# An attention and MLP kernel whose MLP weight splits are kept in DRAM: made in the first token block, loaded in the other three

## The chip, the core and the metric

The kernel runs on one core of one Trainium2 chip. The metric is the device time of one execution in microseconds (us). One core has TensorE (PE: matmuls, with the weight load PEld beside it), VectorE (DVE), ScalarE (ACT), GpSimd (POOL) and SyncE (SP), which here only issues DMAs. Each engine takes its instructions in the order of the program; an instruction that waits for another engine holds up all that stand behind it on its own.

## What is computed

Two branches over the same 2,048 tokens of width 576, mixed by a gate per token:

```python
q, k, v = split(x @ wqkv)              # 32 heads of 18
a = softmax(q @ k.T * 18**-0.5) @ v @ wo
b = gelu(layernorm(x) @ w1 + b1) @ w2 + b2   # 576 -> 4608 -> 576
g = sigmoid((x * gate_w).sum(-1))
out = g * a + (1 - g) * b
```

All is float32. The kernel multiplies with float32r operands and keeps the accuracy by writing an operand as two parts: `hi`, the value rounded to float32r, and `lo`, what is left. A product of two such operands takes three matmuls (hi·hi, hi·lo, lo·hi).

## The kernel before, in words

**Stages.** A first stage (up to about 200 us) makes q, k, v and the layer-normed x (`y_scr`) and stores them in DRAM. Then attention and MLP run interleaved. A last stage multiplies by `wo` and mixes.

**Attention** goes through 32 units (a pair of heads, half of the queries), each in 16 steps: 512 steps. In a step PE makes two rounds of scores for the row maximum (`ps`, L176; DVE reduces them, L178), two pairs of score matmuls (`pss`, L213; four matmuls per step) that ACT turns into exponentials (`p`, L215), and one product with v (L228). `pss` has one buffer, so the next pair waits for the exponential before. At the end of a unit the sums are loaded into a tile `dn` by DMA (L242), and four slots later DVE takes their reciprocal (L251); the negated maxima of the next unit go by DMA from `mr` into two rows of `qa`.

**MLP.** Tokens come in 4 blocks of 512; d_ff = 4608 in 36 chunks of 128, 4 chunks to a group, so 9 groups per block and 18 pairs of chunks. `h_pair(q)` (L339) is 54 matmuls (L350) for a pair of chunks; its result goes through a GELU of five steps shared by ACT (L363, L383, L385) and POOL (`plus`, `parts`: `zz`, `hh`, `hl`, all at line L136), which ends in the two parts `hh` and `hl` of the hidden values. `outs(i)` (L424) is eight `out_unit`s of 24 matmuls (L403) for a group. `outs` waits, by yielding, until the parts of its group stand in `HT` (L429).

**Weights.** A raw pair of w1 is loaded into `r1` (L288), a raw pair of w2 into `r2` (L293), one buffer each. `split` (L301) makes two background jobs of each tile: `first` writes hi on POOL (or ACT for the first ones), `second` subtracts on POOL. The tiles `w` hold both parts: three buffers for w1 (`wp1`), four for w2 (`wp2`). This is done for each of the 72 pairs, that is, for the same 18 pairs four times over.

**What sets the order.** Every step makes four calls of `run_due` (L122); each call is a slot. A slot runs what `defer` put there, and pops one background job from `bg` when the estimated POOL load is under `SLOT`. `fill` (L867) puts MLP pieces into a step until the MLP is as far as its share of the steps, and stops at the end of a unit (`cut` 2) or where the MLP waits (`cut` 3). If a weight tile isn't made when a matmul needs it, `ready` (L313) pops jobs at once; this is called a forced split below. The order of each engine is fixed by this when the program is built. SP issues all loads and stores but those of the output, in this order too.

Of the kernel before, what the change touches and what calls it, by code (L numbers as in the profile page):

```python
# [8 lines left out]
F32 = mybir.dt.float32  # L9
F32R = mybir.dt.float32r  # L10
# [6 lines left out]
P = 128  # L17
S = 2048
D = 576
# [4 lines left out]
NB = 4  # L24
# [4 lines left out]
NFC = F // P  # L29
# [10 lines left out]
WAIT = 0.25  # L40
NSL = 1
SLOT = 950.0
R2 = 1
AHEAD = 1
TOTAL = NB * NG * (G // 2 * 27 * 231 + 8 * 3 * G * 131)
PRO = 36e3
# [11 lines left out]
def gated_mix_kernel(ctx: ExitStack, tc: tile.TileContext, x, wqkv, wo, w1, b1, w2, b2, gate_w, out):  # L58
    nc = tc.nc
# [4 lines left out]
    dram = ctx.enter_context(tc.tile_pool(name="dram", bufs=1, space=DRAM))  # L64
# [3 lines left out]

    qk_scr = dram.tile([2, 2 * D, S], F32, name="qk_scr")
    v_scr = dram.tile([NT, P, NPAIR, VW], F32, name="v_scr")  # L70
    y_scr = dram.tile([NB, 2, 9, 64, TB], F32, name="y_scr")
    ot_scr = dram.tile([2, D, S], F32, name="ot_scr")
    dn_scr = dram.tile([2 * NPAIR, 2, HALF], F32, name="dn_scr")
# [28 lines left out]
    def x_tile():  # L102
        return xp.tile([P, 4 * 640], F32, name="x")
# [4 lines left out]
    def dma_r(queue, dst, src):  # L108

        queue.dma_start(dst.bitcast(F32), src)  # L110


    slot = [0]
    later = []

    def defer(n, fn):
        later.append((slot[0] + n, fn))

    bg = []
    load = [0.0]  # L120

    def run_due():  # L122

        slot[0] += 1
        load[0] = max(load[0] - SLOT, 0.0)
        due = [f for s, f in later if s <= slot[0]]
        later[:] = [(s, f) for s, f in later if s > slot[0]]
        for f in due:
            f()
        if bg and load[0] < SLOT:  # L130
            bg.pop(0)()

    def pool_op(n, fn, *args, **kw):

        load[0] += n * (1.25 if fn == nc.gpsimd.tensor_scalar else 2.55)
        fn(*args, **kw)  # L136
# [132 lines left out]
    def mlp():  # L269
        W1, W2, HT = {}, {}, {}  # L270
        RAW = {}
        seq = [(tb, g) for tb in range(NB) for g in range(NG)]
        n = len(seq)
        npair = n * (G // 2)
        Y, ACC = {}, {}

        def chunk(q):

            i, m = divmod(q, G // 2)
            return i, m, seq[i][1] * G + 2 * m  # L280

        def load_w1(q, view=None):

            r1 = RAW[1, q] = rp.tile([P, 9, P], F32, name="r1") if view is None else view
            fc = chunk(q)[2]
            for h in range(2):
                src = w1[:, (fc + h) * P:(fc + h + 1) * P]
                nc.sync.dma_start(r1[64 * h:64 * h + 64], src.rearrange("(c p) n -> p c n", p=64))  # L288

        def load_w2(q):  # L290
            i, m, fc = chunk(q)
            r2 = RAW[2, q] = rp.tile([P, 2, D], F32, name="r2", bufs=R2)
            nc.sync.dma_start(r2, w2[fc * P:(fc + 2) * P, :].rearrange("(j p) d -> p j d", p=P))  # L293

        def rounded(dst, src, act=False):
# [2 lines left out]
                return  # L298
            pool_op(src.free_size(), nc.gpsimd.tensor_scalar, dst, src, 1.0, 1.0, op0=ALU.mult, op1=ALU.mult)

        def split(table, key, pool, shape, src, act):  # L301

            def first():
                t = table[key, "hi"] = pool.tile(shape, F32R, name=f"w{len(shape)}")
                rounded(t[:, 0], src(), act)

            def second():
                t = table.pop((key, "hi"))
                pool_op(src().free_size(), nc.gpsimd.tensor_tensor, t[:, 1], src(), t[:, 0].bitcast(F32), op=ALU.subtract)
                table[key] = (t[:, 0], t[:, 1])  # L310
            bg.extend([first, second])

        def ready(table, key):  # L313
            while key not in table:
                bg.pop(0)()
            return table[key]

        asked = [1]

        def prep(upto):  # L320

            while asked[0] <= min(upto, npair - 1):
                q = asked[0]
                asked[0] += 1
                split(W1, q, wp1, [P, 2, 9, P], lambda q=q: RAW[1, q], q == 1)
                if q + 1 < npair:
                    bg.append(lambda q=q: load_w1(q + 1))

        def prep_w2(i):
            for m in range(G // 2):  # L330
                q = i * (G // 2) + m
                for j in range(2):
                    split(W2, (q, j), wp2, [P, 2, D], lambda q=q, j=j: RAW[2, q][:, j, :], i == 0)
                if q + R2 < npair:
                    bg.append(lambda q=q: load_w2(q + R2))

        open_pairs = [0]

        def h_pair(q):  # L339

            i, m, fc = chunk(q)
            tb = seq[i][0]
            wt = ready(W1, q)
            del W1[q]
            ps = ps_w.tile([P, 2, TB], F32, name="psw")
            slots = [(w_, 0, c) for c in range(9) for w_ in (0, 1)] + [(0, 1, c) for c in range(9)]
            for k, (w_, s_, c) in enumerate(slots):
                for h in range(2):
                    r = slice(64 * h, 64 * h + 64)
                    nc.tensor.matmul(ps[:, h, :], wt[w_][r, c, :], Y[tb, s_][r, c, :], start=(k == 0), stop=(k == 26))  # L350
                if k == 26:
                    break
                if k % 3 == 2:
                    cut[0] = 1
                yield 231
                while k == 25 and open_pairs[0]:
                    cut[0] = 3
                    yield 0
            open_pairs[0] = 1
            zs = [zp.tile([P, TB], F32, name="z") for _ in range(2)]  # L360
            b = [b1t[:, fc + h:fc + h + 1] for h in range(2)]
            nc.vector.tensor_scalar(zs[1], ps[:, 1, :], b[1], None, op0=ALU.add)
            defer(2, lambda: nc.scalar.activation(zs[0], ps[:, 0, :], AF.Identity, bias=b[0]))  # L363
            for h in (1, 0):
                z = zs[h]
                w = zp.tile([P, TB], F32, name="zz", bufs=2)
                hh = hp.tile([P, TB], F32R, name="hh")
                hl = hp.tile([P, TB], F32R, name="hl")


                def plus(c, w, z):

                    pool_op(TB, nc.gpsimd.tensor_scalar, w, w, c, 1.0, op0=ALU.add, op1=ALU.mult)
                    pool_op(TB, nc.gpsimd.tensor_tensor, w, w, z, op=ALU.mult)

                def parts(w=w, z=z, hh=hh, hl=hl, h=h, j=2 * m + h):
                    plus(1.0, w, z)
                    rounded(hh, w)
                    pool_op(TB, nc.gpsimd.tensor_tensor, hl, w, hh.bitcast(F32), op=ALU.subtract)
                    HT[i, j] = (hh, hl)  # L380
                    if h == 0:
                        open_pairs[0] = 0
                defer(4, lambda w=w, z=z: nc.scalar.activation(w, z, AF.Square))  # L383
                defer(6 - h, lambda w=w, z=z: plus(GC0, w, z))
                defer(10 - 2 * h, lambda w=w: nc.scalar.activation(w, w, AF.Tanh, scale=GC1))  # L385
                defer(11 - 2 * h, parts)
            cut[0] = 2
            yield 231
# [53 lines left out]
        t = [pp.tile([P, 4 * TB], F32R, name="p")[:, :9 * P].rearrange("p (c n) -> p c n", c=9) for _ in range(2)]  # L442
        rounded(t[0], RAW[1, 0])
        nc.gpsimd.tensor_tensor(t[1], RAW[1, 0], t[0].bitcast(F32), op=ALU.subtract)
        W1[0] = t
        yield 1
        load_y(0, 1)
        load_w1(1)
        for q in range(R2):
            load_w2(q)  # L450
        q = 0
        for i in range(n + 1):
            for part in range(2):
# [21 lines left out]
    cut = [0]  # L475
# [15 lines left out]
    def filler(upto):  # L491

        while stream and spent[0] < upto:
            try:
                spent[0] += next(stream[0])
            except StopIteration:
                stream.pop(0)
        run_due()


# [212 lines left out]
    mstack = ExitStack()  # L713
    wp1 = mstack.enter_context(tc.tile_pool(name="m_w1", bufs=3))
    wp2 = mstack.enter_context(tc.tile_pool(name="m_w2", bufs=4))
    rp = mstack.enter_context(tc.tile_pool(name="m_raw", bufs=1))
    zp = mstack.enter_context(tc.tile_pool(name="m_z", bufs=3))

    hooks = []

# [1 line left out]
    def out_proj():  # L722
# [3 lines left out]
        raw = x_tile().rearrange("p (c n) -> p c n", n=640)[:, :, :D]  # L726

        def w_part(hl, c):
            return wbig[:, 5 * hl + c, :] if 5 * hl + c < 8 else wlast[:, c - 3, :]

        def split(c):
            src = raw[:, c % 4, :]
            nc.gpsimd.tensor_scalar(w_part(0, c), src, 1.0, 1.0, op0=ALU.mult, op1=ALU.mult)
            nc.gpsimd.tensor_tensor(w_part(1, c), src, w_part(0, c).bitcast(F32), op=ALU.subtract)
# [3 lines left out]
                nc.sync.dma_start(raw[64 * h:64 * h + 64, 0, :], wo[512:576, :])  # L738

        nc.sync.dma_start(raw, wo[0:512, :].rearrange("(c p) n -> p c n", p=P))  # L740
        bg.append(lambda: split(0))
        bg.append(load_last)
        for c in range(1, 5):
            bg.append(lambda c=c: split(c))
        OT, BT, done = {}, {}, {}

        def load_o(b):
# [73 lines left out]
        for b in range(NB):  # L821
# [7 lines left out]
            for t in range(4):  # L829
# [3 lines left out]
                for n in range(2):  # L833
                    cs = slice(n * ND, (n + 1) * ND)
                    ps = psum(ps_s1)
                    k = 0
# [99 lines left out]
```

## Time and profile before

| what | value |
|---|---|
| median of 3 runs | 2707.01 us (2706.32 to 2707.05) |
| the profiled execution's own time | 2706.99 us |
| its span | 2705.2 us, so 1.8 us lie around it |
| busy: PE, PEld, DVE | 2470.5, 1624.9, 1776.0 us |
| busy: ACT, POOL | 1331.7, 1435.3 us |
| mean granted TensorE clock | 0.955 |
| moved by DMA | 224.21 MB, 83 GB/s over the span |

The page shows the busy time of each engine and its share in 40 equal slices of the span. The group rows give, for a line and an operation, the names (out<-in), the shapes, the count, busy us and mean ns of one, and behind the bar the idle time of the engine just before them with what ended it. The view of waits gives engine, line, what was waited for, us in total, times, and the longest. The view of windows gives, for stretches of the span, the busy us of each engine with its count of instructions (x), the granted clock of TensorE, the share of the DMA engines and GB/s. Rows of the timeline begin with the start in us and the time that they took. Shares of PE are shares of modelled matmul ends; waits are inferred from semaphores.

### The profile page before, as it was taken

The numbers are of one execution on the slowest core, as the hardware profiler recorded it, in microseconds if no ns is written. First come the engines' busy times: TensorE is split into PE (matmuls) and PEld (weight loads), VectorE is DVE, ScalarE is ACT, GpSimd is POOL, SyncE is SP. The second block draws the span as 40 slices with busy tenths as digits, with TensorE's granted clock in tenths as the row PEclk, the third lists the DMA queues.
The fourth block names the chain that finished last, engine by engine and source line by source line (L and its number), as shares of the span: only waits on it lengthen the run. The fifth ranks groups of instructions, "written<-read, shape, count | busy, mean of one in ns | idle before, by whom it ended". The sixth has DMA issues, their size and how long they took to land. (4 is left out here: it accounts for less than half of the span.)

```text
span 2705.2 us, 50403 instructions
## 1 busy us (share of the span) xinstructions
PE 2470.5 (91%) x20585; PEld 1624.9 (60%) x20585; DVE 1776.0 (66%) x3178; ACT 1331.7 (49%) x1555; POOL 1435.3 (53%) x1337
## 2 busy tenths in 40 slices
PE   8996699999978799999978899999889898999868
PEld 7885556666645466666645566656555565666538
DVE  4544567787755577777756677777756676777514
ACT  3221155555545465555535555556545454665541
POOL 3003566675636467556446656566644656666410
PEclk9997799999989899999989999999999999999989
DMA  7676131212261313122251313131442221131145
GB/s 242 210 213 156 44 71 48 67 52 66 53 145 39 75 48 76 47 68 62 53 132 30 76 47 76 48 84 39 97 105 49 64 56 49 50 80 42 34 139 184
DMA packets 210935, 224.21 MB, mean 83 GB/s; under 512 B 55980, under 2 KB 144848, under 8 KB 208976
## 3 DMA queue, kind: packets, MB, share of 16 engines
q1 hardware_dynamic: 208400, 216.27, 30.9%
q10 hardware_dynamic: 2304, 4.72, 0.5%
q8 instruction: 162, 2.65, 0.4%
q14 instruction: 69, 0.57, 0.1%
HBM read 170.61 MB, written 54.26 MB: 83 GB/s over the span
## 5 line engine op out<-in xcount | busy, mean ns | idle before, releaser
L178 DVE TENSOR_REDUCE m<-ps 128x1 f32<-128x512 f32 x2048 | 1290.2, 682 | 393.4 <-PE ps L176 350.1
L215 ACT ACTIVATE p<-pss 128x1024 f32<-128x1024 f32 x1024 | 1049.7, 1025 | 980.8 <-PE pss L213 977.2
L213 PE MATMUL pss<-qa,ka 56*128 56x512 f32 x2048 | 560.0, 411 | 87.2 <-ACT p L215 82.5
L176 PE MATMUL ps<-ka,qa 54*128 54x512 f32 x2048 | 619.8, 454 | 21.7 <-DVE m L178 14.0
L403 PE MATMUL psw<-w,hh 64*128 64x288 f32 x4608 | 542.7, 300 | 52.3 <-POOL hh L136 21.4
L176 PEld LDWEIGHTS ps<-ka,qa 54*128 54x128 f32 x2048 | 311.7, 188 | 460.1 <-DVE x L411 209.6
L228 PE MATMUL ps<-p,vt 128*32 128x512 f32 x4096 | 554.3, 613 | 0.0
L350 PE MATMUL psw<-big,w 64*128 64x512 f32 x3834 | 516.7, 405 | 39.0 <-POOL w L136 27.5
L403 PEld LDWEIGHTS psw<-w,hh 64*128 64x128 f32 x4608 | 492.7, 190 | 81.5 <-POOL hh L136 23.3
L136 POOL TENSOR_SCALAR w<-r 128x576 fp32r<-128x576 f32 (+1 forms) x210 | 175.8, 837 | 604.5 <-DMA r<-in_B_w_dram 373.2
L403 PE MATMUL psw<-w,hl 64*128 64x288 f32 x2304 | 474.9, 299 | 10.6 <-POOL hl L136 10.5
L350 PEld LDWEIGHTS psw<-big,w 64*128 64x128 f32 x3834 | 391.3, 192 | 121.1 <-POOL w L136 32.4
L136 POOL TENSOR_TENSOR w<-r,w 128x576 fp32r<-128x576 f32 (+1 forms) x215 | 393.7, 1832 | 72.5 <-ACT w L297 56.1
L411 DVE SCALAR_TENSOR_TENSOR x<-psw,x 128x288 f32<-128x288 f32 x544 | 248.8, 457 | 248.2 <-PE psw L403 152.4
L403 PEld LDWEIGHTS psw<-w,hl 64*128 64x128 f32 x2304 | 380.4, 190 | 15.1 <-POOL hl L136 14.8
L136 POOL TENSOR_TENSOR zz<-zz,z 128x512 f32<-128x512 f32 x288 | 369.6, 1283 | 24.0
L213 PEld LDWEIGHTS pss<-qa,ka 56*128 56x128 f32 x2048 | 280.5, 189 | 133.8 <-ACT p L215 124.1
L136 POOL TENSOR_SCALAR zz<-zz 128x512 f32<-128x512 f32 x288 | 178.8, 621 | 164.1 <-ACT zz L383 118.9
L136 POOL TENSOR_TENSOR hl<-zz,hh 128x512 fp32r<-128x512 f32 x144 | 187.0, 1298 | 12.0
L228 PEld LDWEIGHTS ps<-p,vt 128*32 128x32 f32 x4096 | 81.3, 108 | 184.1 <-issue 183.9
L385 ACT ACTIVATE zz<-zz 128x512 f32<-128x512 f32 x144 | 89.8, 624 | 92.0 <-POOL zz L136 92.0
L136 POOL TENSOR_SCALAR hh<-zz 128x512 fp32r<-128x512 f32 x144 | 89.4, 621 | 12.6
(97 smaller groups left out, 1279.0 us busy)
## 6 DMA issues: line engine op xcount, KB each, us to landing
r<-in_B_w_dram SPq DMA_DIRECT2D x72, 576.0 KB
r<-in_B_w_dram SPq DMA_DIRECT2D x142, 288.0 KB
big<-y_scr SPq DMA_DIRECT2D x16, 1152.0 KB
qa<-qk_scr SPq DMA_DIRECT2D x192, 72.0 KB
ka<-qk_scr SPq DMA_DIRECT2D x96, 144.0 KB
qk_scr<-hh SPq DMA_DIRECT2D x36, 256.0 KB
qk_scr<-hl SPq DMA_DIRECT2D x36, 256.0 KB
v_scr<-vt SPq DMA_DIRECT2D x16, 416.0 KB
```

Of the source, the lines that this page charges most:

```text
L136: fn(*args, **kw)
L176: nc.tensor.matmul(ps, qa[r0:r0 + 54, t * P:(t + 1) * P], ka[r0:r0 + 54, kb * TB:(kb + 1) * TB], start=True, stop=True)
L178: nc.vector.tensor_reduce(M4[u][:, h, t, kb:kb + 1], ps, axis=AX.X, op=ALU.max)
L213: nc.tensor.matmul(ps[:, h, :], ka[r0:r0 + 56, kc * P:(kc + 1) * P], qa[r0:r0 + 56, qb * TB:(qb + 1) * TB], start=True, stop=True)
L215: nc.scalar.activation(PT[u, kc][:, qb], ps, AF.Exp, scale=SCALE)
L228: nc.tensor.matmul(OB[u][c:c + 32, :], v[:, kc, 19 * h:19 * h + 32], p[:, qb, h, :], start=(kc == 0), stop=(kc == NT - 1))
L350: nc.tensor.matmul(ps[:, h, :], wt[w_][r, c, :], Y[tb, s_][r, c, :], start=(k == 0), stop=(k == 26))
L385: defer(10 - 2 * h, lambda w=w: nc.scalar.activation(w, w, AF.Tanh, scale=GC1))
L403: nc.tensor.matmul(ps[:, h, :ND], h_[r, tok], w_[p_][r, cs], start=(k == 0), stop=(k == 3 * G - 1))
L411: nc.vector.scalar_tensor_tensor(dst, ps[:, h, :ND], 0.5, b2b[:, cs] if g == h == 0 else dst, op0=ALU.mult, op1=ALU.add)
```

## The change

The two parts of each weight pair are made in the first token block only (q below `NQ0` = 18). `second` stores the finished tile in DRAM (`w1_scr`, `w2_scr`); in blocks 2 to 4 `reload` loads a tile, both parts at once, straight into a `w` buffer, with no raw load and no POOL work. A job on a raw tile is popped only `LAND` = 8 slots after its load was issued, and holds up the jobs behind it until then; `ready` doesn't ask for that. The parts of the hidden values are entered in `HT` four slots after their last POOL instruction was issued. `filler` (used before the 512 steps and behind the MLP) stops when the MLP waits. There are four `z` buffers for three.

```diff
-R2 = 1
+LAND = 8
...
+    w1_scr = dram.tile([NFC // 2, P, 2, 9, P], F32, name="w1_scr")
+    w2_scr = dram.tile([NFC, P, 2, D], F32, name="w2_scr")
...
-        if bg and load[0] < SLOT:
-            bg.pop(0)()
+        if bg and load[0] < SLOT and slot[0] >= bg[0][0]():
+            bg.pop(0)[1]()
...
+            LOADED[1, q] = slot[0] + LAND
...
                 pool_op(src().free_size(), nc.gpsimd.tensor_tensor, t[:, 1], src(), t[:, 0].bitcast(F32), op=ALU.subtract)
+                nc.sync.dma_start(scr, t.bitcast(F32))
                 table[key] = (t[:, 0], t[:, 1])
-            bg.extend([first, second])
+            bg.extend([(lambda: LOADED.get(raw, slot[0] + 1), first), (any_time, second)])
+
+        def reload(table, key, pool, shape, scr):
+            t = pool.tile(shape, F32R, name=f"w{len(shape)}")
+            dma_r(nc.sync, t, scr)
+            table[key] = (t[:, 0], t[:, 1])
...
-                split(W1, q, wp1, [P, 2, 9, P], lambda q=q: RAW[1, q], q == 1)
-                if q + 1 < npair:
-                    bg.append(lambda q=q: load_w1(q + 1))
+                shape = [P, 2, 9, P]
+                if q >= NQ0:
+                    reload(W1, q, wp1, shape, w1_scr[q % NQ0])
+                    continue
+                split(W1, q, wp1, shape, (1, q), lambda q=q: RAW[1, q], q == 1, w1_scr[q])
+                if q + 1 < NQ0:
+                    bg.append((any_time, lambda q=q: load_w1(q + 1)))
...
                 for j in range(2):
-                    split(W2, (q, j), wp2, [P, 2, D], lambda q=q, j=j: RAW[2, q][:, j, :], i == 0)
-                if q + R2 < npair:
-                    bg.append(lambda q=q: load_w2(q + R2))
+                    c = 2 * (q % NQ0) + j
+                    if q >= NQ0:
+                        reload(W2, (q, j), wp2, [P, 2, D], w2_scr[c])
+                        continue
+                    split(W2, (q, j), wp2, [P, 2, D], (2, q), lambda q=q, j=j: RAW[2, q][:, j, :], i == 0, w2_scr[c])
+                if q + 1 < NQ0:
+                    bg.append((any_time, lambda q=q: load_w2(q + 1)))
...
-                    HT[i, j] = (hh, hl)
+                    defer(4, lambda: HT.update({(i, j): (hh, hl)}))
...
         nc.gpsimd.tensor_tensor(t[1], RAW[1, 0], t[0].bitcast(F32), op=ALU.subtract)
+        for k in range(2):
+            nc.sync.dma_start(w1_scr[0, :, k], t[k].bitcast(F32))
...
                 stream.pop(0)
+            end, cut[0] = cut[0], 0
+            if end == 3:
+                break
         run_due()
...
-    zp = mstack.enter_context(tc.tile_pool(name="m_z", bufs=3))
+    zp = mstack.enter_context(tc.tile_pool(name="m_z", bufs=4))
```

Two places of the two orders follow, row by row as the engines have them. In the names, `w` is a tile of split weights (128x1152 or 128x2304 wide), `r` a raw tile, `zz`, `hh`, `hl` are steps of the GELU, `w_scr` is either of the two new DRAM tensors.

POOL between two pairs of token block 2, before:

```order
L136 TENSOR_TENSOR hl<-zz,hh 128x512
L136 TENSOR_SCALAR w_9844<-r_9831 128x1152
L136 TENSOR_TENSOR w_9844<-r_9831,w_9844 128x1152
L136 TENSOR_SCALAR w_9906<-r_9899 128x1152
L136 TENSOR_TENSOR w_9906<-r_9899,w_9906 128x1152
L136 TENSOR_SCALAR w_10000<-r_9352 128x576
L136 TENSOR_TENSOR w_10000<-r_9352,w_10000 128x576
L136 TENSOR_SCALAR w_10025<-r_9352 128x576
L136 TENSOR_TENSOR w_10025<-r_9352,w_10025 128x576
L136 TENSOR_SCALAR w_10085<-r_10070 128x576
L136 TENSOR_TENSOR w_10085<-r_10070,w_10085 128x576
L136 TENSOR_SCALAR zz<-zz 128x512
```

The same engine and place now (the line of `pool_op` is L138 there):

```order
L138 TENSOR_SCALAR hh<-zz 128x512
L138 TENSOR_TENSOR hl<-zz,hh 128x512
L138 TENSOR_SCALAR zz<-zz 128x512
L138 TENSOR_TENSOR zz<-zz,z 128x512
L138 TENSOR_SCALAR zz<-zz 128x512
```

Twelve instructions on weights between two pairs' GELUs have gone (ten of them are shown), and the GELU steps follow each other.

SP around the switch from the third to the fourth token block, before (`big` is a part of y for the new block, `mr` the maxima, `b_scr` the finished MLP output):

```order
L288 DMA r_22594<-in_B_w_dram 64x9x128 x2
L288 DMA r_22679<-in_B_w_dram 64x9x128 x2
L293 DMA r_22885<-in_B_w_dram 128x2x576
L293 DMA r_22950<-in_B_w_dram 128x2x576
L110 DMA big<-y_scr 64x9x512 x4
L110 DMA qa_103<-mr 1x8x128 x4
L415 DMA b_scr<-x 128x576
L288 DMA r_23191<-in_B_w_dram 64x9x128 x2
```

SP at this place now:

```order
L112 DMA big<-y_scr 64x9x512 x4
L112 DMA w_22735<-w_scr 128x2304
L112 DMA qa_105<-mr 1x8x128 x4
L439 DMA b_scr<-x 128x576 x2
L244 DMA dn<-oe 128x1x16
...
L439 DMA b_scr<-x 128x576 x2
L112 DMA w_23284<-w_scr 128x1152
L112 DMA w_23286<-w_scr 128x1152
L112 DMA w_23288<-w_scr 128x1152
L112 DMA w_23290<-w_scr 128x1152
L112 DMA w_23384<-w_scr 128x2304
```

The raw loads are gone; a group's four w2 tiles are loaded one after the other once the group before has used its tiles, and the w1 tiles follow one by one.

More of the change, by code (lines that the diff above doesn't have):

```diff
@@ L280, in chunk @@
             return i, m, seq[i][1] * G + 2 * m
+        LOADED = {}
         def load_w1(q, view=None):
             r1 = RAW[1, q] = rp.tile([P, 9, P], F32, name="r1") if view is None else view
+            LOADED[1, q] = slot[0] + LAND
             fc = chunk(q)[2]
@@ L291, in load_w2 @@
             i, m, fc = chunk(q)
-            r2 = RAW[2, q] = rp.tile([P, 2, D], F32, name="r2", bufs=R2)
+            r2 = RAW[2, q] = rp.tile([P, 2, D], F32, name="r2")
+            LOADED[2, q] = slot[0] + LAND
             nc.sync.dma_start(r2, w2[fc * P:(fc + 2) * P, :].rearrange("(j p) d -> p j d", p=P))
@@ L299, in rounded, with any_time, split @@
             pool_op(src.free_size(), nc.gpsimd.tensor_scalar, dst, src, 1.0, 1.0, op0=ALU.mult, op1=ALU.mult)
-        def split(table, key, pool, shape, src, act):
+        def any_time():
+            return 0
+        def split(table, key, pool, shape, raw, src, act, scr):
             def first():
@@ L309, in second @@
                 pool_op(src().free_size(), nc.gpsimd.tensor_tensor, t[:, 1], src(), t[:, 0].bitcast(F32), op=ALU.subtract)
+                nc.sync.dma_start(scr, t.bitcast(F32))
                 table[key] = (t[:, 0], t[:, 1])
-            bg.extend([first, second])
+            bg.extend([(lambda: LOADED.get(raw, slot[0] + 1), first), (any_time, second)])
[3 more added lines that the diff above has]
+            table[key] = (t[:, 0], t[:, 1])
         def ready(table, key):
             while key not in table:
-                bg.pop(0)()
+                bg.pop(0)[1]()
             return table[key]
         asked = [1]
+        NQ0 = npair // NB
         def prep(upto):
@@ L448, in mlp @@
         load_w1(1)
-        for q in range(R2):
-            load_w2(q)
+        load_w2(0)
         q = 0
@@ L740, in out_proj @@
         nc.sync.dma_start(raw, wo[0:512, :].rearrange("(c p) n -> p c n", p=P))
-        bg.append(lambda: split(0))
-        bg.append(load_last)
+        bg.append((lambda: 0, lambda: split(0)))
+        bg.append((lambda: 0, load_last))
         for c in range(1, 5):
-            bg.append(lambda c=c: split(c))
+            bg.append((lambda: 0, lambda c=c: split(c)))
         OT, BT, done = {}, {}, {}
```

## The prediction

> **What bounds the kernel now.** I read the page first. TensorE works nearly all the time:
>
> ```profile
> PE 2470.5 (91%) x20585; PEld 1624.9 (60%) x20585; DVE 1776.0 (66%) x3178; ACT 1331.7 (49%) x1555; POOL 1435.3 (53%) x1337
> PEclk9997799999989899999989999999999999999989
> ```
>
> So a gain can only come from the gaps of PE and from the slices in which its granted clock is under full. To find them I took the start of every attention step from the timeline's L213 rows (four matmuls, so two such rows, a step). First and last of the 511 steps between, and four starts in a quiet place:
>
> ```profile
> 327.42 0.53 PE L213 MATMUL pss<-qa,ka 56*128 56x512 f32 x2
> 2637.55 0.50 PE L213 MATMUL pss<-qa,ka 56*128 56x512 f32 x2
> ...
> 795.67 0.41 PE L213 MATMUL pss<-qa,ka 56*128 56x512 f32 x1
> 799.64 0.40 PE L213 MATMUL pss<-qa,ka 56*128 56x512 f32 x1
> 803.62 0.63 PE L213 MATMUL pss<-qa,ka 56*128 56x512 f32 x2
> ```
>
> A quiet step with one out unit takes 3.97 us. I did the same for each amount of MLP that the code puts into a step (3.3 us with none, 8.65 with a whole pair) and took the fast quarter of each as undisturbed. All 511 steps at those times make 2079.2 us; they take 2310.2. So 231 us are disturbance, and they lie unevenly. The windows view, cut at the switches of the token blocks:
>
> ```profile
> 327.40:764.00 436.60, 425.25 (x3751) 269.40 (x3749) 323.59 (x572) 247.92 (x281) 278.69 (x258) 0.99 0.27 64
> 764.00:819.90 55.90, 42.36 (x355) 24.89 (x355) 32.09 (x61) 23.10 (x26) 22.01 (x22) 0.85 0.61 135
> 819.90:1353.80 533.90, 507.53 (x4438) 322.19 (x4438) 379.25 (x671) 293.20 (x333) 325.44 (x304) 0.97 0.24 59
> 1353.80:1414.60 60.80, 43.41 (x356) 25.95 (x356) 35.50 (x62) 23.08 (x26) 25.93 (x26) 0.83 0.62 135
> 1414.60:1944.50 529.90, 505.01 (x4438) 318.78 (x4438) 379.38 (x670) 293.37 (x333) 329.18 (x307) 0.98 0.25 60
> 1944.50:1995.90 51.40, 41.41 (x356) 24.33 (x356) 34.07 (x63) 23.09 (x26) 22.11 (x22) 0.90 0.70 154
> 1995.90:2540.70 544.80, 509.85 (x4437) 320.80 (x4436) 380.03 (x669) 293.39 (x333) 329.35 (x309) 0.97 0.22 53
> 2540.70:2587.90 47.20, 35.45 (x314) 20.48 (x315) 8.88 (x23) 23.11 (x26) 24.07 (x26) 0.89 0.24 76
> 2587.90:2637.60 49.70, 28.57 (x148) 11.96 (x148) 7.92 (x13) 21.47 (x24) 0.49 (x1) 0.79 0.44 148
> ```
>
> Against undisturbed steps these rows lose, in order: 19.3 (block 1), 17.6, 41.1, 22.5, 38.1, 13.1, 50.3, 9.0 and 20.0 us. Block 1 runs well (clock 0.99). The three rows with 4438 matmuls are the insides of blocks 2 to 4: the same 120 steps, some 493 us undisturbed, 534, 530 and 545 in fact.
>
> What stops PE there is read from waits. Between 2230 and 2260 us, a loss of 12 us:
>
> ```profile
> POOL w L136 <- DMA r<-in_B_w_dram: 22.3, 1, 22.3
> ACT zz L385 <- POOL zz L136: 10.5, 2, 10.0
> PE pss L213 <- ACT p L215: 8.6, 1, 8.6
> ```
>
> This is one chain. POOL stands at `first`, waiting for a raw weight; the GELU step `zz` stands behind it; ACT stands at the tanh that reads `zz`, with the exponentials behind it; PE waits for an exponential. From 825 to 2530 us POOL waits for raw loads 253 us in all; only where such a wait outlasts the slack of the chain does PE stop. The other kind is the forced split, as for pair 20:
>
> ```profile
> POOL w L136 <- DMA r<-in_B_w_dram: 253.4, 26, 22.3
> 848.83 0.79 PE L350 MATMUL psw<-big,w 64*128 64x512 f32 x2 [4.17 <-POOL w L136]
> 851.52 5.06 PE L350 MATMUL psw<-big,w 64*128 64x512 f32 x22 [1.91 <-POOL w L136]
> 778.14 0.80 PE L213 MATMUL pss<-qa,ka 56*128 56x512 f32 x2 [6.91 <-ACT p L215]
> 785.26 0.85 PE L403 MATMUL psw<-w,hh 64*128 64x288 f32 x4 [4.88 <-POOL hh L136]
> ```
>
> The last two rows are a switch of blocks: first the chain again (the loads of y and the raw loads want the DMA engines together), then `outs`, whose `hh` POOL hasn't finished.
>
> **The change, part by part.** The sum is made against the profiled execution's 2706.99 us, of which 2705.2 are span; the median of the runs is 2707.01, the same.
>
> *Insides of blocks 2 to 4.* The splits go. What POOL is spared, by form:
>
> ```profile
> L136 POOL TENSOR_TENSOR w<-r,w 128x576 fp32r<-128x576 f32 x144 | 204.6, 1422 | 15.9 <-ACT w L297 4.8
> L136 POOL TENSOR_TENSOR w<-r,w 128x1152 fp32r<-128x1152 f32 x71 | 189.1, 2663 | 56.6 <-ACT w L297 51.3
> L136 POOL TENSOR_SCALAR w<-r 128x576 fp32r<-128x576 f32 x140 | 94.7, 676 | 344.6 <-DMA r<-in_B_w_dram 182.7 <-PE psw L403 116.2 <-PE pss L213 27.9
> L136 POOL TENSOR_SCALAR w<-r 128x1152 fp32r<-128x1152 f32 x70 | 81.2, 1160 | 259.9 <-DMA r<-in_B_w_dram 190.6 <-PE pss L213 27.7 <-PE ps L176 24.4
> ```
>
> That is three quarters of 570 us, 427 us of POOL; being off PE's path it is worth nothing by itself. What counts is that no raw load stands before a GELU step and no split is forced. The losses of the three insides add up to 129.5 us. Of them 91 us are in steps that lose over 2.1 us each, all but one (3.7 us) with a wait of POOL for a raw load or a forced split in the waits around them: 87 us go. Smaller losses (some 1 us where an out unit follows a pair, which waits for its PSUM buffer) stay for the most part; I take 8 us off. **-95 us** (bounds -70 and -110).
>
> *Switches into blocks 2, 3, 4 and the MLP's end.* `HT` is entered four slots later, so PE does one more step of attention alone (three for two) while POOL finishes `hh` and `hl`. Such a step takes 3.3 us and comes off the end, where the steps without MLP are one fewer, so it is free; it covers 3.3 to 4 of the 4.88 us, and the chain's stall is gone except that block 1's last raw tiles still come and are split by force (switch 1). Switch 1: 17.6 to about 8, **-10**. The other three lose 22.5, 13.1 and about 7 of the 9.0 us; I leave 3 us each: **-33** (bounds -20 and -40).
>
> *Block 1.* It makes what it made, and more stands in its way: each tile is stored too, ahead of the next raw load on SP, and jobs wait 8 slots (two steps, some 8 us) behind a load. By the order, pair 4's w1 and the w2 of groups 1, 2, 4, 7 and 8 are now forced, where before only group 8 had one tile so. A forced w2 pair is four POOL instructions, 2 x (676 + 1422) ns = 4.2 us, behind GELU steps; I take 4 to 5 us of PE for each of five, and 10 us at group 1, where a raw load has to land in between. That is 33 us; the waits for raw loads that `LAND` avoids in this block give back perhaps 8. **+25** (bounds +5 and +50).
>
> [...]
>
> ```profile
> 770.00:792.00 22.00, 9.18 (x52) 4.64 (x46) 3.58 (x7) 4.11 (x5) 15.32 (x16) 0.61 0.94 180
> 437.00:440.00 3.00, 3.00 (x35) 2.06 (x29) 2.81 (x5) 2.00 (x2) 1.74 (x2) 1.00 0.03 6
> ```
>
> Through the stalls of a switch the granted clock was 0.61 on the mean, in a quiet stretch 1.00. [...]
>
> *New loads.* Sizes of what goes and what contends:
>
> ```profile
> r<-in_B_w_dram SPq DMA_DIRECT2D x72, 576.0 KB
> r<-in_B_w_dram SPq DMA_DIRECT2D x142, 288.0 KB
> big<-y_scr SPq DMA_DIRECT2D x16, 1152.0 KB
> L242 SPq DMA_DIRECT2D dn<-oe x32: 590/612/624, 406.1 to 2642.7; - x32
> L251 DVE RECIPROCAL dn<-dn x32: 242/243/254, 408.8 to 2647.5; 128x16 f32<-128x16 f32 x32
> ```
>
> A split tile is twice its raw one: a group now loads 4 x 576 KB for w2 in one burst and 2 x 1152 KB for w1, 4.7 MB. At the 180 GB/s that the y loads show above (share 0.94) the burst takes 13 us; by the order it is asked for seven steps, some 30 us, ahead of use, and w1 eleven or so. The work of two pairs hides it. At a switch, w2 and pair 20's w1 (3.5 MB, 20 us at that rate) have 22 us: tight. The other cost is what is queued behind: the `dn` load is issued 2.7 us before DVE's reciprocal (406.1, 408.8), and row maxima of DVE stand behind that. By the order one burst and four w1 loads stand just ahead of a `dn` load. I take **+8** for both (bounds 0 and +30).
>
> *Before the steps.* Behind a weight not yet landed ACT stood 20.56 us, and PE soon 8.26:
>
> ```profile
> 239.95 1.16 ACT L297 ACTIVATE w<-r 128x1152 fp32r<-128x1152 f32 x1 [20.56 <-DMA r<-in_B_w_dram]
> 260.09 2.07 PE L350 MATMUL psw<-big,w 64*128 64x512 f32 x8 [8.26 <-ACT z L363]
> 279.01 0.61 PE L403 MATMUL psw<-w,hh 64*128 64x288 f32 x2 [5.19 <-POOL w L136]
> ```
>
> `LAND` helps the first, two more stores delay y and group 0's second raw tile. **+3** (bounds -8 and +12). The fourth `z` buffer and the end (20.0 us) I cost at nothing: PE's wait for ACT at `z` was for the PSUM tile, not for `z`.
>
> Sum: -95 - 10 - 33 + 25 + 8 + 3 = -102, so 2707 - 102 = **2605 us**.
>
> **The rivals.**
>
> *Block 1 eats half the gain.* If each store (42.5 MB in 437 us, beside 64 GB/s now) makes raw loads late again, each forced split costs what pair 20's did (8.9 us with its slow clock): eight of them, 71 us in place of 25, and some chains as well: about 2660. For it: raw loads landed up to 22.3 us late even without stores. Against: share 0.27 in block 1.
>
> *The loads don't arrive; slower.* POOL's waits for raw loads become PE's waits for `w` at each of the 27 groups. It costs 8.9 us each as at pair 20, 240 us, so 2605 + 240 = 2845; it turns into a loss from 102/27 = 3.8 us per group. It needs a burst of over 30 us, under 80 GB/s. Against: 180 GB/s in the row above. [...] Here 224 MB become some 330, over 2605 us 127 GB/s, beside 135 to 180 GB/s in rows above.
>
> *No change.* The stalls only move: with POOL free, what lay behind it (ACT, PSUM buffers) stops PE as long. For it: block 1 has the same splits and loses only 19 us, so they alone don't make the loss. Against: the named chains. About 2700.
>
> *A larger gain.* Block 1's forced splits hide behind attention, and the smaller losses go too: the optimistic bounds, -110 - 15 - 40 + 5 - 8, give about 2540 to 2570.
>
> **How the numbers follow.** The forecast with its own spread (2570 to 2640) 0.68; block 1 eating half (2640 to 2690) 0.15; the larger gain 0.10; no change 0.02; slower 0.05. What a measurement of this kernel can tell from no change is about 0.2%, 5 us. The range takes the forecast and the nearer part of the first rival: 2570 to 2655. Faster 0.93, same 0.02, slower 0.05.
>
> **What would show it.** Right: POOL's waits for raw loads end at the first switch; the three insides take 500 to 510 us each with the clock at 0.99 or more; POOL near 1010 us busy; about 330 MB moved; block 1 longer than 436.6 us, with PE waiting for POOL `w` at L403's line. Wrong: PE waits for DMA `w` in blocks 2 to 4, or DVE for `dn`; insides over 515 us; block 1 over 480.

## The result, and the profile after

The changed kernel takes 2600.42 us (median of 4 runs, 2594.74 to 2605.15), the kernel before 2706.66 us beside it (4 runs): a ratio of 0.961, 95% interval 0.9588 to 0.9631. Forecast were 2605 us, in 2570 to 2655.

The profiled execution has a span of 2598.1 us, 107.1 less than before. The busy times on its page:

```profile
PE 2451.8 (94%) x20585; PEld 1606.4 (62%) x20585; DVE 1772.8 (68%) x3178; ACT 1331.8 (51%) x1555; POOL 1005.4 (39%) x1013
PEclk9998689999999999999999999999999999999989
DMA packets 163559, 330.38 MB, mean 127 GB/s; under 512 B 56860, under 2 KB 83520, under 8 KB 152512
```

POOL is 430 us less busy; PE, DVE and ACT do the same work as before. In the insides of blocks 2 to 4 the granted clock is full (1.00 in the rows below, 0.97 to 0.98 before). The bytes grew by half, the packets fell by a fifth.

The windows view, cut at the same switches as before (columns as there):

```profile
332.00:797.20 465.20, 435.69 (x3751) 271.16 (x3749) 326.13 (x572) 248.06 (x281) 274.27 (x256) 0.96 0.46 133
797.20:844.10 46.90, 40.31 (x331) 22.72 (x331) 31.23 (x59) 23.13 (x26) 17.61 (x19) 0.93 0.78 185
844.10:1350.00 505.90, 500.50 (x4461) 316.88 (x4462) 379.34 (x673) 293.14 (x333) 194.74 (x205) 1.00 0.33 107
1350.00:1391.20 41.20, 37.71 (x332) 21.80 (x333) 31.77 (x60) 23.12 (x26) 13.57 (x15) 1.00 0.75 159
1391.20:1895.90 504.70, 499.32 (x4462) 315.94 (x4462) 379.35 (x672) 293.31 (x333) 194.69 (x205) 1.00 0.33 108
1895.90:1936.60 40.70, 38.42 (x331) 22.29 (x329) 33.08 (x61) 23.08 (x26) 13.59 (x15) 0.96 0.70 162
1936.60:2444.90 508.30, 501.29 (x4459) 315.69 (x4458) 379.53 (x671) 293.45 (x333) 194.77 (x205) 1.00 0.29 99
2444.90:2484.70 39.80, 32.72 (x289) 18.23 (x289) 8.16 (x21) 23.15 (x26) 23.86 (x25) 0.91 0.27 83
2484.70:2532.00 47.30, 29.78 (x170) 13.33 (x170) 8.84 (x15) 21.74 (x24) 0.74 (x1) 0.78 0.48 161
```

The insides of blocks 2 to 4 take 506, 505 and 508 us where they took 534, 530 and 545. Each switch is shorter (55.9, 60.8, 51.4 and 47.2 us before). Block 1 is longer: 465.2 for 436.6.

Who waits in block 1, and who for a raw weight in the rest. First the view of waits from 332 to 797 us, then the one from 844 to 1350 us, the inside of block 2, its first rows:

```profile
POOL w L138 <- DMA r<-in_B_w_dram: 78.1, 6, 27.6
PEld psw L427 <- POOL w L138: 30.4, 21, 7.0
PE psw L427 <- POOL w L138: 24.8, 19, 6.8
```

```profile
POOL zz L138 <- ACT zz L407: 254.5, 13, 33.6
ACT p L217 <- PE pss L215: 209.4, 231, 5.7
DVE m L180 <- PE ps L178: 66.2, 68, 3.5
```

From block 2 on POOL waits for ACT's next GELU step, that is, it has nothing to do; waits for raw loads end with block 1. ACT waits for PE. In block 1 PE waits 25 us for POOL's `w` at the out units' line (L427 here), where the same stretch before had 4.3 us.

### The profile page after: what moved, and what is told of

Same layout as the page of the kernel before. It is cut to its first block, busy times and chain, and to the rows that moved or that the text cites. A ratio compares the mean times of both kernels' runs of the same rounds, so it can differ in the third digit from the quotient of the medians.

```text
span 2598.1 us, 50271 instructions
## 1 busy us (share of the span) xinstructions
PE 2451.8 (94%) x20585; PEld 1606.4 (62%) x20585; DVE 1772.8 (68%) x3178; ACT 1331.8 (51%) x1555; POOL 1005.4 (39%) x1013
## 4 chain that ended last, share of the span: by engine, by line
PE 75%; POOL 10%; issue 4%; DMA 4%; DVE 3%; ACT 2%; SPq 1%; POOLq 0%; ACTq 0%; DVEq 0%
PE ps L230 16%; PE psw L427 15%; PE ps L178 14%; PE psw L374 14%; PE pss L215 8%; POOL zz L138 4%; PE ps L645 4%; POOL w L138 2%; POOL hl L138 2%; ACT p L217 2%; PE ps L665 2%; DMA r<-in_B_w_dram 1%; PE ps L869 1%; DVE m L180 1%; POOL hh L138 1%
## 5 line engine op out<-in xcount | busy, mean ns | idle before, releaser
L217 ACT ACTIVATE p<-pss 128x1024 f32<-128x1024 f32 x1024 | 1049.9, 1025 | 943.5 <-PE pss L215 938.2
L178 PE MATMUL ps<-ka,qa 54*128 54x512 f32 x2048 | 618.9, 454 | 20.7 <-DVE m L180 10.5
L427 PE MATMUL psw<-w,hh 64*128 64x288 f32 x4608 | 544.7, 301 | 53.9 <-POOL w L138 32.7
L215 PE MATMUL pss<-qa,ka 56*128 56x512 f32 x2048 | 553.0, 407 | 18.0 <-ACT p L217 12.9
L138 POOL TENSOR_SCALAR zz<-zz 128x512 f32<-128x512 f32 x288 | 178.3, 619 | 980.4 <-ACT zz L407 931.1
L427 PEld LDWEIGHTS psw<-w,hh 64*128 64x128 f32 x4608 | 494.4, 190 | 86.6 <-POOL w L138 40.3
L374 PE MATMUL psw<-big,w 64*128 64x512 f32 x3834 | 502.4, 397 | 10.3 <-POOL w L138 6.4
L427 PE MATMUL psw<-w,hl 64*128 64x288 f32 x2304 | 473.9, 298 | 9.0 <-POOL hl L138 9.0
L374 PEld LDWEIGHTS psw<-big,w 64*128 64x128 f32 x3834 | 376.6, 187 | 92.9 <-ACT z L387 9.6
L427 PEld LDWEIGHTS psw<-w,hl 64*128 64x128 f32 x2304 | 380.2, 189 | 12.4 <-POOL hl L138 12.1
L138 POOL TENSOR_TENSOR zz<-zz,z 128x512 f32<-128x512 f32 x288 | 369.5, 1283 | 24.0
L215 PEld LDWEIGHTS pss<-qa,ka 56*128 56x128 f32 x2048 | 277.6, 187 | 61.4 <-ACT p L217 52.0
L138 POOL TENSOR_TENSOR hl<-zz,hh 128x512 fp32r<-128x512 f32 x144 | 187.0, 1298 | 12.0
L138 POOL TENSOR_TENSOR w<-r,w 128x576 fp32r<-128x576 f32 (+1 forms) x53 | 96.0, 1812 | 65.1 <-ACT w L303 61.1
L645 PE MATMUL ps<-big,wh 128*128 128x512 f32 x288 | 93.5, 406 | 2.3 <-ACT wh L567 2.3
L138 POOL TENSOR_SCALAR hh<-zz 128x512 fp32r<-128x512 f32 x144 | 89.1, 619 | 12.6
```

Source lines behind the costliest of these rows:

```text
L178: nc.tensor.matmul(ps, qa[r0:r0 + 54, t * P:(t + 1) * P], ka[r0:r0 + 54, kb * TB:(kb + 1) * TB], start=True, stop=True)
L215: nc.tensor.matmul(ps[:, h, :], ka[r0:r0 + 56, kc * P:(kc + 1) * P], qa[r0:r0 + 56, qb * TB:(qb + 1) * TB], start=True, stop=True)
L217: nc.scalar.activation(PT[u, kc][:, qb], ps, AF.Exp, scale=SCALE)
L427: nc.tensor.matmul(ps[:, h, :ND], h_[r, tok], w_[p_][r, cs], start=(k == 0), stop=(k == 3 * G - 1))
L645: nc.tensor.matmul(ps, w_[:, c, ms], big[:, s_, :], start=(k == 0), stop=False)
```

## The experiments

Losses below are worked out as in the prediction: step lengths from the L215 or L217 rows of score matmuls, less the undisturbed length of a step with the same MLP work (the same lengths throughout). The unit is us. The median is of four or five executions, the columns behind the ratio are from the profiled one alone (e2's is the slowest of its four, 2608 us, e5's the fastest of its four, 2739 us). The changed kernel, e4, e5 and e6 have the same order up to the first reloads, late in block 1, so their rows show how far executions differ: the steps begin at 327 to 332 us and block 1 loses 48 to 52 us.

| kernel | median | ratio to before (95%) | first step at | block 1 | into 2 | inside 2, 3, 4 | into 3, 4, end |
|---|---|---|---|---|---|---|---|
| before | 2706.66 | 1 | 327.4 | 19.3 | 17.6 | 41.1, 38.1, 50.3 | 22.5, 13.1, 9.0 |
| changed | 2600.42 | 0.961 (0.9588–0.9631) | 332.0 | 47.9 | 9.3 | 11.1, 10.8, 10.9 | 3.6, 3.1, 2.2 |
| e1_no_reload | 2810.27 | 1.0375 (1.0359–1.039) | 325.7 | 41.0 | 9.3 | 61.7, 76.6, 94.5 | 14.0, 8.8, 5.6 |
| e2_land0 | 2603.3 | 0.9608 (0.9592–0.9624) | 341.3 | 38.2 | 12.7 | 9.9, 10.7, 10.8 | 6.2, 4.6, 0.9 |
| e3_ht_now | 2618.36 | 0.9669 (0.9655–0.9684) | 330.3 | 48.6 | 12.3 | 10.0, 10.9, 9.5 | 8.5, 8.7, 8.1 |
| e4_pool_busy | 2602.44 | 0.9607 (0.9593–0.9622) | 328.0 | 49.9 | 8.9 | 12.7, 11.6, 11.6 | 4.9, 3.2, 0.3 |
| e5_pool_wait | 2748.69 | 1.0143 (1.0116–1.0171) | 327.2 | 51.2 | 12.8 | 50.0, 45.2, 53.9 | 16.3, 9.2, 0.4 |
| e6_load_twice | 2810.21 | 1.0376 (1.0351–1.0401) | 328.9 | 52.2 | 9.4 | 72.5, 68.6, 64.8 | 24.2, 25.6, 0.3 |
| e7_store_twice | 2619.61 | 0.9671 (0.9654–0.9687) | 329.8 | 62.9 | 9.9 | 14.9, 10.9, 11.0 | 4.8, 3.2, 1.1 |
| e8_store_pool | 2614.12 | 0.9659 (0.9629–0.9689) | 331.7 | 58.7 | 11.0 | 10.6, 10.9, 10.9 | 4.8, 3.3, -0.3 |
| e9_store_later | 2594.27 | 0.9585 (0.9572–0.9598) | 331.0 | 42.1 | 8.9 | 12.1, 11.0, 11.0 | 4.8, 3.2, -0.4 |
| e10_land_early | 2593.53 | 0.9589 (0.9573–0.9604) | 331.1 | 43.2 | 11.6 | 10.5, 11.0, 10.9 | 3.6, 3.2, -0.3 |
| e11_both | 2587.8 | 0.9561 (0.954–0.9582) | 329.5 | 33.7 | 13.8 | 10.7, 10.9, 10.9 | 3.6, 3.2, -0.4 |
| e12_land46 | 2582.64 | 0.954 (0.9526–0.9554) | 328.8 | 27.1 | 13.6 | 13.7, 10.8, 10.9 | 3.6, 3.2, -0.4 |

**e1_no_reload: the change without its DRAM copy.** Splits in all blocks, the rest as changed.

```diff
-                nc.sync.dma_start(scr, t.bitcast(F32))
...
-                if q >= NQ0:
-                    reload(W1, q, wp1, shape, w1_scr[q % NQ0])
-                    continue
...
-                    if q >= NQ0:
-                        reload(W2, (q, j), wp2, [P, 2, D], w2_scr[c])
-                        continue
```

> All four blocks make their own splits, as before; landing distance, late entry in HT and the rest of the change stay. Theory (the loads in place of the splits are the gain; a distance of 8 slots gets rid of waits for raw tiles but brings forced splits): the insides of blocks 2 to 4 lose about as much as block 1 does now (48 us less what the stores cost, so 25 to 45 us each in place of 11), the switches stay short: 2650 to 2700 us. Rival (the landing distance alone is the gain, the DRAM copy is ballast): 2580 to 2610 us.

It took 2810 us, 100 more than the kernel before: both expectations missed. The rival is out. With splits in every block the rest of the change is a loss, and by the waits it is the landing distance that costs (no run has splits in every block without the distance):

```profile
POOL w L138 <- DMA r<-in_B_w_dram: 275.0, 25, 31.4
PE psw L420 <- POOL w L138: 106.8, 85, 4.3
PE psw L367 <- POOL w L138: 69.6, 17, 14.6
PE pss L215 <- ACT p L217: 19.7, 22, 5.8
```

The chain over tanh and exponentials is nearly gone (20 us for PE), as the distance intends, but PE waits 176 us for `w` itself: jobs held back by 8 slots are then split by force. POOL's wait for raw loads is shorter than before the change (275 us for 373), but far from gone: `ready` pops a job without asking for the distance. Why the loss grows from block to block wasn't tried.

**e4_pool_busy: POOL's time given back, the waiting not.** In blocks 2 to 4 POOL multiplies old raw tiles, in the shapes and number of the splits; nothing reads the products.

```diff
+        def spend(view):
+            def one():
+                pool_op(view.free_size(), nc.gpsimd.tensor_scalar, view, view, 1.0, 1.0, op0=ALU.mult, op1=ALU.mult)
+            def two():
+                pool_op(view.free_size(), nc.gpsimd.tensor_tensor, view, view, view, op=ALU.mult)
+            bg.extend([(any_time, one), (any_time, two)])
...
                     reload(W1, q, wp1, shape, w1_scr[q % NQ0])
+                    spend(RAW[1, NQ0 - 1])
...
                         reload(W2, (q, j), wp2, [P, 2, D], w2_scr[c])
+                        spend(RAW[2, NQ0 - 1][:, j, :])
```

> The changed kernel, and POOL does in blocks 2 to 4 the same amount of work as the splits were, in the same places of the background queue, on raw tiles that have long been there and that nobody reads any more: POOL is as busy as before (about 1435 us) and never waits for a load. Theory (waiting for raw tiles and forced splits are the cost, POOL's time is not): 2600 to 2625 us. Rival (POOL's load is the cost: GELU steps queue behind splits): 2660 to 2700 us.

2602 us, with POOL as loaded as before but for 63 us:

```profile
PE 2450.1 (94%) x20585; PEld 1601.4 (62%) x20585; DVE 1777.4 (68%) x3178; ACT 1331.8 (51%) x1555; POOL 1371.8 (53%) x1337
```

366 us of POOL work cost 2 us, less than runs differ. The gain is not POOL's time.

**e5_pool_wait: the waiting given back, POOL's time not.** In blocks 2 to 4 each raw pair is loaded too, and one instruction on 32 columns reads it.

```diff
+        def touch(key, load):
+            def one():
+                t = RAW[key].rearrange("p a b -> p (a b)")
+                pool_op(1152, nc.gpsimd.tensor_scalar, t[:, 0:32], t[:, 0:32], 1.0, 1.0, op0=ALU.mult, op1=ALU.mult)
+            bg.extend([(any_time, load), (any_time, one)])
...
+                    touch((1, q), lambda q=q: load_w1(q))
...
+                        if j == 1:
+                            touch((2, q), lambda q=q: load_w2(q))
```

> The changed kernel, and in blocks 2 to 4 each raw pair is loaded as well, with one small POOL instruction (32 columns) behind each load that reads it one slot after the load was asked for: POOL waits for raw tiles again but has no split to do and no weight hangs on it. Theory (the wait at POOL's head, passed on to tanh, exponentials and PE, is the cost): 50 to 90 us come back, 2650 to 2690 us, with waits of POOL for raw tiles of about 200 us. Rival (the forced splits and POOL's time were the cost): 2600 to 2620 us.

2749 us: the losses of the insides are back at 45 to 54 us, at and above those of before, with POOL 1026.0 us busy, 346 less than in e4. More than the theory gave. Its waits:

```profile
POOL r L138 <- DMA r<-in_B_w_dram: 1004.6, 90, 45.6
ACT zz L418 <- POOL zz L138: 136.1, 41, 16.3
PE pss L215 <- ACT p L217: 110.3, 36, 15.0
PE pss L215 <- DMA qa<-mr: 8.5, 5, 3.1
```

The chain stands there row by row: POOL for the raw tile, the tanh for POOL, PE for the exponential behind the tanh, 110 us (12.9 us in the changed kernel). POOL's wait is far longer than in the kernel before (373 us): the small instruction stands one slot behind its load, and the raw loads come on top of the reloads (394 MB in all). So the run gives the mechanism and not its size in the kernel before. That the added bytes alone made the loss doesn't fit: PE waits for no reload, and for `mr` only 8.5 us.

**e3_ht_now: hidden values entered at once.**

```diff
-                    defer(4, lambda: HT.update({(i, j): (hh, hl)}))
+                    HT[i, j] = (hh, hl)
```

> The changed kernel with the hidden values entered in HT at once, as before. Theory (the later entry covers the 4 to 5 us for which PE waited for hh at each of four switches): one attention step less there, the wait is back: 2 to 5 us at each, 2608 to 2620 us, with PE waits for POOL hh at the out units' line. Rival (the switches are short only because the raw loads are gone): 2595 to 2603 us.

2618 us, as the theory had it. The switches lose 8 to 12 us in place of 2 to 9. PE's waits for `hh` in this kernel, then in the changed one:

```profile
PE psw L427 <- POOL hh L138: 12.1, 3, 4.8
```

```profile
PE psw L427 <- POOL hh L138: 3.3, 3, 1.5
```

So of the change's 107 us some 17 (the spans are 2615.4 and 2598.1) hang on these four slots, and 19 of the 44 us that the switches gained.

**e6_load_twice: have the loads room?** Every reload done twice into the same tile.

```diff
             dma_r(nc.sync, t, scr)
+            dma_r(nc.sync, t, scr)
```

> The changed kernel with every reload done twice into the same tile: 9.4 MB a group in place of 4.7. Theory (the loads have room: a burst has some 30 us and takes under 13): the double burst takes up to 26 us and just fits, a few losses at the switches and at dn: 2600 to 2630 us. Rival (the loads are near the limit): each of 27 groups loses 4 us or more, over 2710 us.

2810 us: the theory is wrong and the rival's size is right, 210 us over 27 groups, 7.8 us each. The view of waits, with SP's own first, and behind it, from the windows view, the stretch of the worst one (switch to block 2, pair 20):

```profile
SPq L112 <- DMA w<-w_scr: 884.0, 173, 22.1
DVE dn L253 <- DMA dn<-oe: 53.1, 11, 13.3
PE psw L375 <- DMA w<-w_scr: 44.9, 3, 21.7
PE pss L215 <- DMA qa<-mr: 41.2, 7, 19.4
PE psw L428 <- DMA w<-w_scr: 24.8, 8, 5.5
```

```profile
872.00:895.00 23.00, 1.43 (x7) 1.25 (x9) 0.93 (x2) 2.12 (x3) 6.29 (x7) 0.59 0.63 230
```

But the edit does more than double the bytes. The second load writes the tile that the first one writes, and SP holds it back until the first has landed: 884 us of waiting at the head of SP's queue, of which the changed kernel has none. So the tiles are loaded one after the other, and whatever stands behind them on SP stands too: the weights come late (70 us for PE), and so do `dn` and `mr`, a few KB each (53 us for DVE, 41 us for PE). In the worst stretch the DMA engines were 0.63 busy, not full. In the changed kernel DVE waits 1.6 us for `dn`, and PE never for `w<-w_scr`. So the run shows what a wait at the head of SP's queue does to the small transfers behind it; whether twice the bytes alone would have had room is not shown.

**e2_land0: no landing distance.** `LAND = 0`.

> The changed kernel with a landing distance of 0 slots. It can only touch block 1 and what lies ahead of it. Theory A (block 1's loss comes from splits that the distance has made late): the forced splits go, block 1 loses some 20 to 25 us in place of 48: 2570 to 2585 us. Theory B (the stores make raw loads late, the distance protects the GELU chain from that): waits of POOL for raw tiles come back, block 1 loses 50 to 70 us: 2605 to 2630 us.

2603 us, neither: block 1 and the stretch into block 2 lose 6 us less in sum, but the steps begin at 341.3 in place of 332.0. That start is later than in every other run here (325.7 to 332.0), but it is from one execution, and the waits don't explain it: from 200 us to the first step ACT and POOL wait 44 us for raw weights without the distance and 57 us with it. So the distance costs where jobs pile up; how it would help ahead of the steps is not shown.

**e7_store_twice and e8_store_pool: what the stores cost.** A second store of each tile to a DRAM tile that nobody reads; and stores asked for by POOL.

```diff
                 nc.sync.dma_start(scr, t.bitcast(F32))
+                nc.sync.dma_start(again(scr), t.bitcast(F32))
```

```diff
-                nc.sync.dma_start(scr, t.bitcast(F32))
+                nc.gpsimd.dma_start(scr, t.bitcast(F32))
```

> The changed kernel with every finished tile of block 1 stored a second time, to a DRAM tile that nobody reads. Theory (block 1's extra loss of 29 us is in part the stores, which stand ahead of the next raw load): 8 to 25 us more, all in block 1: 2608 to 2625 us. Rival (the loss is the order of the splits alone): 2597 to 2604 us.

> The changed kernel with block 1's stores asked for by POOL behind its own split in place of SP, so that no later load on SP waits for a split. If SP's waiting for the splits (228 us in the trace) makes raw loads late: block 1 loses 15 to 25 us less, 2575 to 2590 us. If not, or if asking costs POOL about 1 us each time: 2600 to 2620 us.

A second set of stores costs block 1 15 us (62.9 for 47.9). Not all of that need be their bytes: they go to one DRAM tile for each shape, so SP also waits for the store before to land, in SP's own view of waits:

```profile
SPq L325 <- DMA w_two<-w: 85.2, 17, 18.3
```

What the first set costs is seen more directly in e1, without stores: block 1 loses 41.0 us, 7 less. Asked for by POOL the stores cost block 1 11 us more than by SP, not less (2614 us; the ratio's interval just touches the changed kernel's). POOL spends 53 x 0.6 us on asking, in the engine that the forced splits wait for (29 us of PE's wait for `w` in block 1 against 25). The stores' issues on POOL (min/median/max ns), and the row of waits:

```profile
L319 POOL DMA_DIRECT2D w_scr<-w x53: 571/602/747, 248.0 to 827.6; - x53
```

```profile
PE psw L427 <- POOL w L138: 29.2, 25, 5.1
```

**e9 to e12: mending block 1.** Stores 8 slots later, behind the next raw load (e9); the landing distance ahead of the steps only (e10); both (e11); both, with the distance only up to slot 46 (e12). The edit of e12 is shown; e10 and e11 have 80 in place of 46, e9 has the first part alone, e10 the second, and `load_w2` is changed as `load_w1` is.

```diff
-                nc.sync.dma_start(scr, t.bitcast(F32))
+                defer(8, lambda: nc.sync.dma_start(scr, t.bitcast(F32)))
...
-            LOADED[1, q] = slot[0] + LAND
+            LOADED[1, q] = slot[0] + (LAND if slot[0] < 46 else 0)
```

> The changed kernel with each store of block 1 asked for 8 slots after its split, so that the next raw load stands ahead of it on SP. Theory (a store costs because the next raw load waits behind its bytes): block 1 loses 38 to 42 us in place of 48, the stretch ahead of the steps is some 5 us shorter: 2585 to 2595 us. Rival (the stores cost as bytes beside other transfers, wherever they stand): 2597 to 2605 us.

> The changed kernel with the landing distance of 8 slots only ahead of the 512 steps (slots up to 79), and none in them. Theory (the distance pays ahead of the steps, 9 us, and costs 10 us in block 1, which is why 0 and 8 came out alike): start of the steps as with 8, block 1 as with 0: 2588 to 2596 us. Rival (0 and 8 are alike everywhere, what differed was chance): 2598 to 2605 us.

> Both of the above: stores 8 slots later, and no landing distance in the steps. Theory: the two add up, block 1 loses 25 to 32 us: 2572 to 2588 us. Rival (they mend the same thing): as the better one of the two, 2588 to 2597 us.

> As the one with both, but the landing distance ends at slot 46, ahead of the first out units, so that group 1's first w2 pair and pair 4 of w1 are no longer split by force (the loss of 14 us in step 5). Theory: 5 to 10 us less than the one with both: 2565 to 2580 us. Rival (without the distance group 0's raw tiles hold up POOL ahead of the steps): 2585 to 2600 us.

2594, 2594, 2588 and 2583 us. e9 and e10 each take 5 to 6 us off block 1 as the changed kernel has it (47.9), though their intervals touch the changed kernel's. e9's 42.1 is what its theory gave; e10's 43.2 lies halfway to the 38.2 without any distance, so its theory holds in the total and only half in block 1. In e11 block 1 loses 33.7, more saved than the two savings in sum (14 us for 11), but the stretch into block 2 gives 4 back, and its time ends on the border of theory and rival. e12 is 5 us under e11, as its theory had it, but 3 us above the range. Its ratio 0.954 (0.9526 to 0.9554) lies clear below the changed kernel's 0.961 (0.9588 to 0.9631), though not of e11's. Its median is the lowest here, and block 1 loses 27 us, 8 more than before the change.

## Why the prediction was right, point by point

- **Insides of blocks 2 to 4**, -95 forecast: losses 129.5 before, 32.8 after, so -96.7. The reason holds by two runs: the time of POOL alone costs nothing (e4: 366 us of it, 2 us more), POOL waiting alone stops PE through tanh and exponentials (e5: 110 us of waits of PE). How much was this chain and how much forced splits was not tried, but the waits give a share: in the three insides PE waited 37.8 us for exponentials and 28.1 us for POOL's `w` before, and 1.6 and 0 us now. The rest of the 96.7 (lower clock, smaller waits) is not split up. The fourth `z` buffer and the stop in `filler` were costed at nothing and not tried alone.
- **Switches**, -10 and -33 forecast: -8.3 and -35.7. Somewhat under half of it, 19 of 44 us, hangs on the later entry in `HT` (e3). That the extra step of attention is free was slightly wrong: the undisturbed lengths of the steps as now filled add up to 5 us more than before.
- **Block 1**, +25 forecast: +28.6. The prediction named six forced splits: the w2 of groups 1, 2, 4, 7 and 8, and pair 4's w1. The trace has PE waiting for POOL's `w` at these five groups, and for under 2 us at 3, 5 and 6 too, but not at pair 4's w1; group 8's falls behind the switch. The prediction also took it that before only group 8 was forced; PE waited 4.3 us at group 1 then already. The largest, group 1, from the timeline of the changed kernel, POOL first, then PE:

```profile
362.05 0.67 POOL L138 TENSOR_SCALAR w<-r 128x576 fp32r<-128x576 f32 x1 [6.65 <-DMA r<-in_B_w_dram]
```

```profile
355.46 0.40 PE L427 MATMUL psw<-w,hh 64*128 64x288 f32 x2 [1.09 <-POOL w L138]
362.78 0.61 PE L427 MATMUL psw<-w,hh 64*128 64x288 f32 x2 [6.79 <-POOL w L138]
```

  The step lost 14.2 us, 6.8 more than before; 10 more were taken. The steps with the forced splits of groups 2, 4 and 7 lost 6 to 7 us each where 4 to 5 were taken. Behind a stop of 1.09 us two matmuls took 0.40 us, behind one of 6.79 us 0.61, and the granted clock of the next 4.2 us was 0.50. Before, it was 0.50 too from 851.52 to 856.38 us, behind pair 20's waits of 4.17 and 1.91 us: the slow clock in the prediction's 8.9 us. How much of block 1's loss is the lower clock was not split off. The size of +25 rested on pieces that were off in both directions: the stores, taken as no term of their own, cost some 7 us (e1's block 1, without them, loses 41.0), and relief of 8 us by the landing distance was not there: with it block 1 loses 5 to 10 us more than without (e10, e2).
- **New loads**, +8 forecast, up to +30: nothing to be seen, 1.6 us of DVE for `dn`. With SP held up by its own loads (e6, 884 us) just the transfers that the prediction named, `dn`, `mr` and pair 20's `w`, came late, so it looked at the right queue; how many bytes the slower rival would need is not shown. Here 106 MB more went with 107 us less, at 99 to 108 GB/s in the insides.
- **Before the steps**, +3: the first step starts 4.6 us later. In e4, e5 and e6, whose order is the same there, it starts at 328.0, 327.2 and 328.9, for 327.4 before, so the 4.6 us are not clear of what executions differ by. The relief by `LAND` wasn't there: ACT's longest wait for a raw weight is 21.4 us, 20.6 before. **The end**, 0: 3 us less lost, and 1.5 us less behind the steps.

Sum: -96.7 - 8.3 - 35.7 + 28.6 + 4.6 - 3.0 - 1.5 + 5 = -107.0; the spans differ by 107.1. That the total came within 5 us of the forecast is in part luck: the loads, the end, block 1 and the longer undisturbed steps were off by -8, -4.5, +3.6 and +5 us, which largely cancelled. The two large terms, insides and switches, were right in size by themselves.

Of the rivals, that block 1 would eat half did not come (47.9 us lost, not 90). No change is out. One part of the change is a loss where it was taken as a help: the landing distance inside the steps (e1, e10, e12).

## What to carry to other kernels

Look not at how busy a helper engine is but at what stands behind its waits in its own queue: here 366 us of extra POOL work cost nothing, and small instructions that waited for loads cost over 100 us. A background job held back to spare a queue must still be done before its user forces it; hold back only where there is slack. When work is replaced by loads, look at what stands behind them in the queue of the engine that issues them: where SP had to wait before it could issue the next load (e6), transfers of a few KB came late as well, and were waited for as long as the late weights (53 us by DVE and 41 us by PE, beside 70 us by PE for the weights).

## What the runs showed that was not expected

Reloads moved more with less of the DMA engines' time than the loads of y: a stretch of the changed kernel with them, and the stretch of y loads before, quoted in the prediction (0.94, 180):

```profile
858.00:870.00 12.00, 11.86 (x96) 6.89 (x92) 7.05 (x12) 7.58 (x11) 8.10 (x9) 1.00 0.71 270
```

270 GB/s at a share of 0.71. A reload's run in DRAM is 9,216 or 4,608 bytes for each partition, that of y 2,048 bytes; whether that is the reason was not tried. So the bound that the prediction took from the y loads, 13 us for a burst, was on the safe side.
